# Attention and two expert layers on one core: the first batch's sums of four and its pooled part move from VectorE into TensorE's products

## The chip, the cores and the metric

The kernel runs on one core of a Trainium2 chip. The metric is the device time of one execution in microseconds (us). TensorE (PE, with its weight loads as PEld), VectorE (DVE), ScalarE (ACT), GpSimd (POOL) and SyncE (SP) each run their own instructions in order; DMA transfers are issued on queues of SP and of ACT.

## The reference, cut to what matters

```python
# q, k, v: 4 batches x 8 heads x 576 tokens x 64
q_d, k_d, v_d = (t.reshape(B, H, 144, 4, D).mean(axis=3) for t in (q, k, v))
out_d = softmax(scale * q_d @ k_d^T) @ v_d                 # 144 pooled tokens
out_up = np.repeat(out_d, 4, axis=2)                       # the pooled part, back on 576
mask = np.abs(pos[:, None] - pos[None, :]) < 4
out_local = softmax(where(mask, scale * q @ k^T, -1e9)) @ v
x = (out_up + out_local) as [2304 tokens, 512]
x = ((x @ w_a) * (x @ w_b)) @ w_out                        # 512 -> 1536 -> 512
h = x @ w_in                                               # 512 -> 2048
out = (h * clip(h + 3, 0, 6) / 6) @ w_out2                 # 2048 -> 512
```

## The kernel before, in words

The program has three phases, each of which a small list scheduler writes out: `Plan` (lines 57 to 135) holds steps with an engine, an estimated duration, a due time (`want`), the steps they follow, and the tags they take and give back (buffers and banks, with caps). It simulates the engines and calls each step's function in the order in which it would start, and each engine then runs its instructions in that order; on the chip only the order counts. Changed durations, due times or takes therefore change the order around them too.

Phase 1 makes x and multiplies it with w_a and w_b. The 2304 tokens are cut into units of 116 tokens (five to a batch, the last of 112), and the units into seven token blocks of 2, 3, 3, 3, 3, 3 and 3 units. `BUFS` (line 175) gives two score tiles `s2` of two PSUM banks each and four single banks `b`; the cap `pv` lets one result of a value product at a time hold one of those four.

`pooled(b, g, want)` does the pooled attention of one pair of heads g of batch b, four groups to a batch. `load` brings queries and keys (tile qk), `load_v` the values as four slices, one for each of the four neighbours of a pooled token. `add_v` (lines 375 to 379) adds the four slices with two DVE instructions. `sums` (381 to 384) adds four neighbouring queries and keys in one DVE reduce, into dqk. `score` (386 to 393, result dsc) multiplies summed queries with summed keys on PE, four F32 matmuls of two instructions each. `top` takes the maxima (line 397) and scales them (400), `exps` is on ACT (406), `inverse` (412, 413) and `norm` (345) on DVE; `turn` transposes on PE (424, dpt), `turned` copies on ACT (431, deT), `pv` (434 to 439, dpo) multiplies with the added values, and `keep` (444) writes the result to od.

`local(u, want)` does the windowed attention of unit u in the same steps: `score` (mask at 479, products at 485, result sc), `top` (493, 494), `exps` (501; eight heads in one step), `inverse`, `norm`, `turn` (516), `turned` (520), and `pv` (528; 32 instructions into po, each with its own start). `total` (536) adds the pooled part from od, each value repeated four times, into xf on DVE; `x_first` (543, ACT) and `x_second` (546, DVE) split xf into a rounded part and its remainder, tile x, as PE multiplies those in pairs.

`decode` (223 to 280) turns one slab of weights, 128x1024 numbers of 64 bits (raw), into two such parts (wh): ACT at line 237, DVE at 243, 244, 248, 254, 255 and 261, ACT at 265, DVE at 268. `job(n, f)` (568) multiplies block n with slab f: 12 products of w_a and 12 of w_b (578, pab), their product on ACT and DVE (584, 587), and the store. The first six jobs are blocks 0 to 2 with the slabs 0 and 1; then come the slabs from 2 on with the blocks 0 to 2, and later the other blocks. The first two slabs are loaded by ACT's queue (lines 945 and 946 give `queue=nc.scalar`), the others by SP's.

Phase 2 multiplies with w_out, and phase 3 is the second expert layer.

## Time and profile before

| | us |
|---|---|
| median of 3 runs (lowest, highest) | 973.01 (971.87, 974.76) |
| the profiled execution | 975.95 |
| its span, first to last instruction | 974.2 |
| PE busy in the span | 927.7 |
| DVE busy | 766.0 |
| ACT busy | 457.3 |

How to read it: the span is one execution as the profiler recorded it; the difference to that execution's time lies around the program. Busy times overlap, as the engines work side by side. PEclk is the clock that PE was granted, as a share of full speed. A wait in brackets at a row's end is the idle time of that engine just before the row, and what ended it.

### The profile page before, as it was taken

The page shows a single profiled execution, that of the slowest core. Times are in us where ns is not written, and L with a number is a line of the kernel's source. Part 1 is how long each engine was busy: PE and PEld are TensorE (multiplying, and loading weights), DVE is VectorE, ACT ScalarE, POOL GpSimd, SP SyncE. Part 2 cuts the span into 40 slices and gives each one's busy share as a digit, 9 for nine tenths or more (in the row PEclk, how much of TensorE's full clock was granted, in tenths as well). Part 3 has the DMA queues.
Part 4 walks back from the last instruction along what each step waited for, and adds up shares of the span by engine and source line. Part 5 has one row for each costly group of instructions (what it writes and reads, how often), then busy time and mean ns, then how long its engine had stood idle before and what let it go on. Part 6 is the DMA issues. An engine that isn't in the chain of part 4 may idle for free.

```text
span 974.2 us, 18526 instructions
## 1 busy us (share of the span) xinstructions
PE 927.7 (95%) x7040; PEld 869.7 (89%) x7040; DVE 766.0 (79%) x1390; ACT 457.3 (47%) x1164; POOL 5.2 (1%) x44
## 2 busy tenths in 40 slices
PE   3779999999999999999999898999999999999998
PEld 2568899999989999997877688999999999999998
DVE  6888898954746959686887644899898999997983
ACT  3765633445455424224444333545454665554551
POOL 1000000000000000000000000000000000000000
PEclk9988999999999999999999899999999999999999
DMA  8442755323314433325678664334327891815401
GB/s 259 173 122 82 243 163 192 127 84 99 112 49 132 169 136 133 131 95 204 214 241 271 219 211 147 104 142 164 122 108 256 274 295 43 265 39 167 159 17 49
DMA packets 90089, 151.21 MB, mean 155 GB/s; under 512 B 8208, under 2 KB 71696, under 8 KB 85648
## 3 DMA queue, kind: packets, MB, share of 16 engines
q1 hardware_dynamic: 80384, 132.54, 41.4%
q10 hardware_dynamic: 9616, 17.49, 5.7%
q8 instruction: 55, 0.90, 0.4%
q14 instruction: 34, 0.28, 0.1%
HBM read 100.19 MB, written 49.81 MB: 154 GB/s over the span
## 4 chain that ended last, share of the span: by engine, by line
PE 80%; DVE 9%; DMA 7%; ACT 2%; issue 2%; ACTq 0%; SPq 0%; DVEq 0%
PE pab L578 32%; PE ph L747 16%; PE oacc L870 15%; PE acc L635 9%; DMA h<-h_d 4%; PE po L528 2%; DVE in L678 2%; DMA vz<-vt 1%; PE sc L485 1%; PE pt L516 1%; PE dpo L439 1%; DVE e L843 1%; DVE w2o L1078 1%; PE dpt L424 1%; DMA raw<-wab 1%
## 5 line engine op out<-in xcount | busy, mean ns | idle before, releaser
L578 PE MATMUL pab<-x,wh 128*128 128x344 f32 (+2 forms) x2016 | 325.6, 320 | 1.9 <-DVE wh L268 1.7
L578 PEld LDWEIGHTS pab<-x,wh 128*128 128x128 f32 x2016 | 311.8, 192 | 4.7 <-DVE wh L268 2.0
L870 PE MATMUL oacc<-w2o,in 128*128 128x256 f32 x1512 | 182.1, 283 | 1.4 <-DVE in L678 1.4
L870 PEld LDWEIGHTS oacc<-w2o,in 128*128 128x128 f32 x1512 | 181.3, 191 | 2.2 <-DVE in L678 2.0
L747 PE MATMUL ph<-in,w 128*128 128x384 f32 x1008 | 177.3, 337 | 2.5 <-ACT in L675 2.3
L747 PEld LDWEIGHTS ph<-in,w 128*128 128x128 f32 x1008 | 176.7, 189 | 3.0 <-ACT in L675 2.5
L635 PE MATMUL acc<-h,wo 128*128 128x512 f32 (+1 forms) x720 | 156.5, 377 | 9.4 <-ACT h L623 8.3
L635 PEld LDWEIGHTS acc<-h,wo 128*128 128x128 f32 x720 | 126.7, 191 | 39.2 <-ACT h L623 10.8
L763 DVE TENSOR_TENSOR part<-ph,part 128x384 f32<-128x384 f32 x168 | 85.7, 549 | 9.6 <-PE ph L747 8.8
L584 ACT ACTIVATE a<-pab 128x344 f32<-128x344 f32 (+2 forms) x84 | 37.3, 447 | 95.8 <-PE pab L578 67.5
L771 ACT ACTIVATE r<-part,three 128x384 f32<-128x384 f32 x96 | 56.5, 613 | 52.9 <-DVE part L763 50.1
L587 DVE TENSOR_TENSOR a<-a,pab 128x344 f32<-128x344 f32 (+2 forms) x84 | 41.4, 493 | 50.3 <-PE pab L578 45.2
L627 DVE TENSOR_TENSOR h<-h 128x512 fp32r<-128x512 f32 (+1 forms) x60 | 37.4, 634 | 51.6 <-ACT h L623 51.3
L675 ACT ACTIVATE in<-gr 128x384 fp32r<-128x384 f32 x96 | 47.5, 521 | 41.0 <-PE oacc L870 31.2
L237 ACT ACTIVATE m<-raw 128x1024 f32<-128x1024 f32 x34 | 39.3, 1157 | 57.0 <-DVE raw L255 21.2
L623 ACT ACTIVATE h<-h 128x512 fp32r<-128x512 f32 (+1 forms) x60 | 34.9, 588 | 64.5 <-DMA h<-h_d 51.6
L678 DVE TENSOR_TENSOR in<-gr,in 128x384 fp32r<-128x384 f32 x96 | 49.5, 551 | 6.7 <-ACT in L675 6.2
L675 ACT ACTIVATE in<-e 128x384 fp32r<-128x384 f32 x72 | 36.5, 527 | 33.9 <-PE oacc L870 20.2
L774 DVE SCALAR_TENSOR_TENSOR r<-r,part 128x384 f32<-128x384 f32 x96 | 50.4, 548 | 1.2 <-ACT r L771 1.1
L501 ACT ACTIVATE e<-sc,mx 128x64 f32<-128x64 f32 x160 | 47.6, 328 | 5.5 <-DVE mx L494 4.4
L255 DVE SCALAR_TENSOR_TENSOR raw<-raw,m 128x1024 f32<-128x1024 uint32 x34 | 41.7, 1227 | 1.2
L261 DVE TENSOR_TENSOR raw<-raw 128x1024 f32<-128x1024 f32 x34 | 41.5, 1221 | 0.5
(82 smaller groups left out, 885.7 us busy)
## 6 DMA issues: line engine op xcount, KB each, us to landing
g_d<-r SPq DMA_DIRECT2D x96, 192.0 KB
gr<-g_d SPq DMA_DIRECT2D x48, 384.0 KB
h<-h_d ACTq DMA_DIRECT2D x48, 256.0 KB
raw<-wab SPq DMA_DIRECT2D x10, 1024.0 KB
h_d<-a SPq DMA_DIRECT2D x48, 172.0 KB
raw<-w2i SPq DMA_DIRECT2D x8, 1024.0 KB
raw<-w2o SPq DMA_DIRECT2D x8, 1024.0 KB
qk<-qk SPq DMA_DIRECT2D x14, 576.0 KB
```

The source lines that it names most:

```text
L255: nc.vector.scalar_tensor_tensor(out=lo.bitcast(F32), in0=lo, scalar=2.0 ** -52, in1=m, op0=ALU.mult, op1=ALU.mult)
L261: nc.vector.tensor_tensor(v, v, lo.bitcast(F32), op=ALU.add)
L501: nc.scalar.activation(e[:, p, h], L["s4"][:, p, h], AF.Exp, bias=L["mx"][:, p, h:h + 1], scale=SCALE, accum_out=z[:, p, h:h + 1])
L578: nc.tensor.matmul(T[k], wab_t[f][:, x, c], xs[n][:, g, y, :nb], start=(g == 0 and i == 0), stop=(g == KC - 1 and i == 2))
L635: nc.tensor.matmul(accs[n][e], wo_t[f // 2][:, x, c], hs[n, f][:, y], start=(f == 0 and i == 0), stop=(f == F1 - 1 and i == 2))
L675: nc.scalar.activation(x[0][:, 0], src(), AF.Copy)
L678: nc.vector.tensor_tensor(x[0][:, 1], src(), x[0][:, 0], op=ALU.subtract)
L747: nc.tensor.matmul(acc[k], t[:, x, g * P:(g + 1) * P], X[k, g][0][:, y], start=(g == 0 and n == 0), stop=(g == 1 and n == 2))
L763: nc.vector.tensor_tensor(s[name], acc[k], s[other], op=ALU.add)
L771: nc.scalar.activation(T["r"], src(), AF.Relu, bias=three)
L774: nc.vector.scalar_tensor_tensor(out=T["r"], in0=T["r"], scalar=6.0, in1=src(), op0=ALU.min, op1=ALU.mult)
L870: nc.tensor.matmul(acc[n][e], X[n, k][0][:, x, e * P:(e + 1) * P], t[:, y], start=(k == 0 and i == 0), stop=(k == K - 1 and i == 2))
```

## The change

For batch 0 (`soon` in `pooled`): the four value slices aren't added, and `pv` multiplies with each of them into the same bank (16 matmuls in place of 4). DVE sums the keys alone (128x144 in place of 128x288 results), and `score` takes the four query slices as weights one after another, read with a step of four numbers (16 matmuls in place of 4). For the units of 116 tokens in blocks 0 to 2 (seven units; `soon` in `local`): `pv` begins with one product of the identity with the pooled part, read from od with each column four times (128x464), the 32 others add to it, `total` isn't done, and `x_first` and `x_second` read PSUM. For every unit the exponentials are four steps of two. The first two slabs of w_a and w_b go on SP's queue. Some durations, due times and takes of the planner change with it.

```diff
--- before.py
+++ after.py
@@ -353 +353 @@
-    def pooled(b, g, want):
+    def pooled(b, g, want, soon):
@@ -377 +377 @@
-            T["v"] = v_[:, :, 0] if b == 0 else slot(ap, [HD, 2, P], F32, "dv", "dv")
+            T["v"] = slot(ap, [HD, 2, P], F32, "dv", "dv")
@@ -380,0 +381,3 @@
+        def tokens():
+            return qks[b, g][:, :, HALO:HALO + S].rearrange("p a (s r) -> p a s r", r=FACTOR)
@@ -381,0 +385,2 @@
+            a = slice(1, 2) if soon else slice(0, 2)
@@ -383,2 +388 @@
-            nc.vector.tensor_reduce(T["s"], qks[b, g][:, :, HALO:HALO + S].rearrange("p a (s r) -> p a s r", r=FACTOR),
-                                    axis=AX.X, op=ALU.add)
+            nc.vector.tensor_reduce(T["s"][:, a], tokens()[:, a], axis=AX.X, op=ALU.add)
@@ -390,4 +394,6 @@
-                for h in range(2):
-                    r = slice(64 * h, 64 * h + 64)
-                    nc.tensor.matmul(sc[:HD, h, a * SD:(a + 1) * SD], s[r, 0, a * HD:(a + 1) * HD], s[r, 1],
-                                     start=True, stop=True)
+                part = slice(a * HD, (a + 1) * HD)
+                for i in range(FACTOR if soon else 1):
+                    for h in range(2):
+                        r = slice(64 * h, 64 * h + 64)
+                        nc.tensor.matmul(sc[:HD, h, a * SD:(a + 1) * SD], tokens()[r, 0, part, i] if soon else s[r, 0, part],
+                                         s[r, 1], start=(i == 0), stop=(not soon or i == FACTOR - 1))
@@ -435,0 +442,2 @@
+            v = [T["v_"][:, :, i] for i in range(FACTOR)] if soon else [T["v"]]
@@ -437,3 +445,5 @@
-                for h in range(2):
-                    r = slice(64 * h, 64 * h + 64)
-                    nc.tensor.matmul(po[r, :SD], T["v"][:, c, r], T["eT", c][:, h], start=(c == 0), stop=(c == 1))
+                for i, x in enumerate(v):
+                    for h in range(2):
+                        r = slice(64 * h, 64 * h + 64)
+                        nc.tensor.matmul(po[r, :SD], x[:, c, r], T["eT", c][:, h], start=(c == 0 and i == 0),
+                                         stop=(c == 1 and i == len(v) - 1))
@@ -449,2 +459,2 @@
-        av = DVE(dve(768) + 0.06, want - 3, add_v, [lv], take=[] if b == 0 else ["dv"], give=[] if b == 0 else ["vraw"])
-        i = DVE(dve(2 * S), want, sums, [ld], take=["dqk"])
+        av = lv if soon else DVE(dve(768) + 0.06, want - 1, add_v, [lv], take=["dv"], give=["vraw"])
+        i = DVE(dve(S if soon else 2 * S), want, sums, [ld], take=["dqk"])
@@ -452 +462 @@
-        i = PE(0.5, want, score, [i], take=["s2"], give=["dqk"])
+        i = PE(2.0 if soon else 0.5, want, score, [i], take=["s2"], give=["dqk"])
@@ -454 +464 @@
-        i = ACT(4 * 0.47, want, exps, [i], take=["de"], give=["s2"])
+        i = ACT(4 * 0.37, want, exps, [i], take=["de"], give=["s2"])
@@ -457,4 +467,5 @@
-        t = [PE(0.3, want, turn(c), [i], take=["b", "turn"], give=["de"] if c else []) for c in range(2)]
-        t = [ACT(act(2 * SD), want, turned(c), [t[c]], take=["deT"], give=["b", "turn"]) for c in range(2)]
-        i = PE(0.6, want, pv, [*t, av], take=["b", "pv"], give=["deT", "deT", "wh" if b == 0 else "dv"])
-        S_["od", b, g] = ACT(act(SD), want, keep, [i, S_.get(("od", b, 0))], take=[] if g else ["od"], give=["b", "pv"])
+        t = [PE(0.3, want, turn(c), [i], take=["b", "turn", "deT"], give=["de"] if c else []) for c in range(2)]
+        t = [ACT(act(2 * SD), want, turned(c), [t[c]], give=["b", "turn"]) for c in range(2)]
+        i = PE(1.6 if soon else 0.6, want, pv, [*t, av], take=["b", "pv"] + ([] if g else ["od"]),
+               give=["deT", "deT", "wh" if b == 0 else "vraw" if soon else "dv"])
+        S_["od", b, g] = ACT(act(SD), want, keep, [i, S_.get(("od", b, 0))], give=["b", "pv"])
@@ -462 +473 @@
-    def local(u, want):
+    def local(u, want, soon):
@@ -496,4 +507,5 @@
-        def exps():
-            e = L["e"] = slot(ap, [P, HP, 2, KB], F32, "e", "e")
-            z = L["z"] = ap.tile([P, HP, 2], F32, tag="z", bufs=2, name="z")
-            for p in range(HP):
+        def exps(p):
+            def run():
+                if p == 0:
+                    L["e"] = slot(ap, [P, HP, 2, KB], F32, "e", "e")
+                    L["z"] = ap.tile([P, HP, 2], F32, tag="z", bufs=2, name="z")
@@ -501,2 +513,3 @@
-                    nc.scalar.activation(e[:, p, h], L["s4"][:, p, h], AF.Exp, bias=L["mx"][:, p, h:h + 1],
-                                         scale=SCALE, accum_out=z[:, p, h:h + 1])
+                    nc.scalar.activation(L["e"][:, p, h], L["s4"][:, p, h], AF.Exp, bias=L["mx"][:, p, h:h + 1],
+                                         scale=SCALE, accum_out=L["z"][:, p, h:h + 1])
+            return run
@@ -524,0 +538,2 @@
+            if soon:
+                nc.tensor.matmul(L["po"].rearrange("p a (s r) -> p a s r", r=FACTOR), ident, pooled_part(), start=True, stop=False)
@@ -529 +544,4 @@
-                                         L["eT"][:, p, i * KB:i * KB + QB], start=True, stop=True)
+                                         L["eT"][:, p, i * KB:i * KB + QB], start=not soon,
+                                         stop=(not soon or (p == HP - 1 and i == 1)))
+            if soon:
+                L["xf"] = L["po"]
@@ -531,2 +549 @@
-        def total():
-            xf = L["xf"] = slot(ap, [P, HP, UT], F32, "xf", "xf")
+        def pooled_part():
@@ -535 +552,4 @@
-            up = ods[b][:, :, c:c + n].unsqueeze(3).to_broadcast([P, HP, n, FACTOR])
+            return ods[b][:, :, c:c + n].unsqueeze(3).to_broadcast([P, HP, n, FACTOR])
+        def total():
+            xf = L["xf"] = slot(ap, [P, HP, UT], F32, "xf", "xf")
@@ -537 +557,2 @@
-                                    L["po"][:, :, :tokens].rearrange("p a (s r) -> p a s r", r=FACTOR), up, op=ALU.add)
+                                    L["po"][:, :, :tokens].rearrange("p a (s r) -> p a s r", r=FACTOR), pooled_part(),
+                                    op=ALU.add)
@@ -549 +570 @@
-        ld = DMA(128, want - 25 if u < 2 else want - 5, load, [S_.get(("pv", u - 2))])
+        ld = DMA(128, want - 20 if u < 2 else want - 5, load, [S_.get(("pv", u - 2))])
@@ -555 +576,2 @@
-        i = ACT(8 * 0.42, want, exps, [i], take=["e"], give=["s2"])
+        for p in range(HP):
+            i = ACT(2 * 0.31, want, exps(p), [i], take=[] if p else ["e"], give=["s2"] if p == HP - 1 else [])
@@ -558,5 +580,7 @@
-        i = PE(0.5, want, turn, [i], take=["b", "turn"], give=["e"])
-        i = ACT(act(n), want, turned, [i], take=["eT"], give=["b", "turn"])
-        i = S_["pv", u] = PE(0.9, want, pv, [i, ld], take=["b", "pv"], give=["eT"])
-        i = DVE(dve(n), want, total, [i] + [S_["od", b, g] for g in range(HP)], take=["xf"],
-                give=["b", "pv"] + (["od"] if last else []))
+        i = PE(0.5, want, turn, [i], take=["b", "turn", "eT"], give=["e"])
+        i = ACT(act(n), want, turned, [i], give=["b", "turn"])
+        ods_ = [S_["od", b, g] for g in range(HP)]
+        i = S_["pv", u] = PE(1.7 if soon else 0.9, want, pv, [i, ld] + ods_,
+                             take=["b", "pv"] + ([] if soon else ["xf"]), give=["eT"])
+        if not soon:
+            i = DVE(dve(n), want, total, [i], give=["b", "pv"] + (["od"] if last else []))
@@ -565 +589 @@
-        S_["x2", u] = DVE(dve(n), want, x_second, [i], give=["xf"])
+        S_["x2", u] = DVE(dve(n), want, x_second, [i], give=["b", "pv"] if soon else ["xf"])
@@ -941,2 +965,2 @@
-                pooled(u // NU, g, t - 0.05 + 0.01 * g)
-        local(u, t)
+                pooled(u // NU, g, t - 0.05 + 0.01 * g, u // NU < 1)
+        local(u, t, m < 3 and unit_tokens(u) == UT)
@@ -946 +970 @@
-                                queue=nc.scalar if f < 2 else None)
+                                queue=None)
```

SP's queue at the start of the program (v0 are the value slices of batch 0, raw the slabs of weights, vz the values of a unit, qk the queries and keys, those of batch 1 here). Before:

```order
L370 DMA v0_146<-vd 72x1024
L370 DMA v0_156<-vd 72x1024
L370 DMA v0_161<-vd 72x1024
L370 DMA v0_178<-vd 72x1024
L473 DMA vz0_105<-vt 64x512 x2
L473 DMA vz1_106<-vt 64x512 x2
L365 DMA qk_279<-qk 128x2x576
L365 DMA qk_303<-qk 128x2x576
```

With the change:

```order
L370 DMA v0_176<-vd 72x1024
L370 DMA v0_183<-vd 72x1024
L370 DMA v0_210<-vd 72x1024
L370 DMA v0_215<-vd 72x1024
L229 DMA raw_248<-wab 128x1024
L229 DMA raw_312<-wab 128x1024
L484 DMA vz0_105<-vt 64x512 x2
L484 DMA vz1_106<-vt 64x512 x2
L365 DMA qk_391<-qk 128x2x576
```

The two slabs, which ACT's queue issued before, stand between the values of batch 0 and those of the first two units.

PE's first rows (dsc is a pooled score, dpt a transpose of its exponentials, dpo the pooled product with the values, sc a unit's score; qk_113, qk_117, qk_121 and the last one are the four groups of batch 0). Before:

```order
L392 MATMUL dsc<-dqk 72x144 x16
L424 MATMUL dpt<-ident,de 72x72 x8
L439 MATMUL dpo<-deT,v_146 64x144 x4
L424 MATMUL dpt<-ident,de 72x72 x4
L479 LDWEIGHTS ident_88
L479 MATMUL sc<-mask_sb,ident_88 128x256
...
L485 MATMUL sc<-qk_132 64x64 x4
L424 MATMUL dpt<-ident,de 72x72 x4
L439 MATMUL dpo<-deT,v_156 64x144 x4
```

With the change:

```order
L398 MATMUL dsc<-dqk,qk_113 72x144 x16
L398 MATMUL dsc<-dqk,qk_117 72x144 x16
L398 MATMUL dsc<-dqk,qk_121 72x144 x16
L430 MATMUL dpt<-ident,de 72x72 x4
L490 LDWEIGHTS ident_88
L490 MATMUL sc<-mask_sb,ident_88 128x256
...
L496 MATMUL sc<-qk_144 64x64 x4
L430 MATMUL dpt<-ident,de 72x72 x4
L448 MATMUL dpo<-deT,v_176 64x144 x16
L398 MATMUL dsc<-dqk,qk_144 72x144 x16
```

Before, one row holds the scores of all four groups; with the change each group has a row, and the fourth stands behind a unit's score and the first group's product with the values.

DVE's rows behind the second pooled maximum's (dmx) scale, up to the maximum of the fourth group. Before:

```order
L383 TENSOR_REDUCE dqk<-qk_132 128x288
L378 TENSOR_TENSOR v_146<-v_146 72x2x256
L379 TENSOR_TENSOR v_146<-v_146 72x2x128
L378 TENSOR_TENSOR v_156<-v_156 72x2x256
L379 TENSOR_TENSOR v_156<-v_156 72x2x128
L345 TENSOR_TENSOR de<-de,dz 72x576
L378 TENSOR_TENSOR v_161<-v_161 72x2x256
L379 TENSOR_TENSOR v_161<-v_161 72x2x128
L378 TENSOR_TENSOR v_178<-v_178 72x2x256
L379 TENSOR_TENSOR v_178<-v_178 72x2x128
...
L397 TENSOR_REDUCE dmx<-dsc 72x4
```

With the change:

```order
L345 TENSOR_TENSOR de<-de,dz 72x576
L388 TENSOR_REDUCE dqk<-qk_144 128x144
...
L403 TENSOR_REDUCE dmx<-dsc 72x4
L406 TENSOR_SCALAR dmx<-dmx 72x4
L345 TENSOR_TENSOR de<-de,dz 72x576
L504 TENSOR_REDUCE mx<-sc 128x8
L505 TENSOR_SCALAR mx<-mx 128x8
...
L345 TENSOR_TENSOR de<-de,dz 72x576
L403 TENSOR_REDUCE dmx<-dsc 72x4
```

The eight rows of value adds are gone, the sum is half as large, and the first unit's maximum (mx) and a third norm (de) stand ahead of the fourth group's maximum. Behind PE's row 370 or so (377 with the change), and DVE's 404 (389), the two orders are the same on every engine.

## Rows read from the trace of the kernel before

**Rows 1.** The page: one engine's busy time, share of the span, instructions.

```profile
PE 927.7 (95%) x7040; PEld 869.7 (89%) x7040; DVE 766.0 (79%) x1390; ACT 457.3 (47%) x1164; POOL 5.2 (1%) x44
```

**Rows 2.** Windows: stretch and its length in us, busy time by engine, clock, DMA.

```profile
core 0: us, PE busy (x) PEld busy (x) DVE busy (x) ACT busy (x) POOL busy (x), PEclk, DMA share, GB/s
0.00:30.00 30.00, 12.53 (x104) 8.15 (x104) 18.51 (x35) 10.40 (x42) 3.97 (x28) 1.00 0.91 284
6.00:22.70 16.70, 8.02 (x52) 5.45 (x53) 13.91 (x26) 5.20 (x26) 0.00 (x0) 1.00 0.98 262
22.70:54.30 31.60, 21.75 (x304) 15.64 (x307) 27.36 (x53) 22.13 (x95) 0.00 (x0) 0.95 0.55 184
54.30:114.70 60.40, 55.36 (x670) 49.24 (x662) 52.52 (x96) 37.98 (x164) 0.64 (x8) 0.88 0.41 130
114.70:442.00 327.30, 327.30 (x2789) 315.21 (x2790) 240.31 (x388) 138.78 (x405) 0.64 (x8) 1.00 0.39 128
```

**Rows 3.** Timeline of the start: us, duration, engine, line, work [idle before it <-releaser].

```profile
5.32 2.85 DVE L383 TENSOR_REDUCE dqk<-qk 128x288 f32<-128x1152 f32 x2 [4.46 <-DMA qk<-qk]
6.73 0.80 PEld L392 LDWEIGHTS dsc<-dqk 64*72 64x72 f32 x8 [6.73 <-DVE dqk L383]
6.73 1.24 PE L392 MATMUL dsc<-dqk 64*72 64x144 f32 x8 [6.73 <-DVE dqk L383]
...
21.78 0.75 DVE L397 TENSOR_REDUCE dmx<-dsc 72x4 f32<-72x576 f32 x1
...
26.91 1.12 ACT L237 ACTIVATE m<-raw 128x1024 f32<-128x1024 f32 x1 [3.58 <-DMA raw<-wab]
...
28.06 0.69 DVE L243 TENSOR_SCALAR m<-m 128x1024 f32<-128x1024 f32 x1 [2.55 <-ACT m L237]
```

**Rows 4.** The chain of waits, pieces in order of time: start us, us, what.

```profile
18.95 7.94 DMA raw<-wab
...
28.32 1.44 ACT de L406 x8
...
62.43 0.64 PE dsc L392 x8
...
75.90 1.96 PE pab L578 x12
...
85.89 0.67 PE sc L485 x32
```

**Rows 5.** Timelines of PE and DVE around two cuts, the x halves of units 1 and 7.

```profile
43.51 1.96 PE L528 MATMUL po<-eT,vz 128*64 128x58 f32 x32 [0.69 <-ACT eT L520]
...
47.94 1.16 PE L528 MATMUL po<-eT,vz 128*64 128x58 f32 x32
...
53.74 0.59 DVE L546 TENSOR_TENSOR x<-xf,x 128x464 fp32r<-128x464 f32 x1
...
114.00 0.63 DVE L546 TENSOR_TENSOR x<-xf,x 128x464 fp32r<-128x464 f32 x1
...
114.69 1.55 PE L578 MATMUL pab<-x,wh 128*128 128x348 f32 x8 [0.16 <-DVE x L546]
```

**Rows 6.** Tiles v, qk and xf: duration ns min/median/max, first and last start us, forms.

```profile
L378 DVE TENSOR_TENSOR v<-v x4: 679/680/681, 15.1 to 18.9; 72x512 f32<-72x512 f32 x4
L379 DVE TENSOR_TENSOR v<-v x4: 420/420/422, 15.8 to 19.6; 72x256 f32<-72x256 f32 x4
...
L383 DVE TENSOR_REDUCE dqk<-qk x10: 1319/1344/1354, 5.3 to 126.6; 128x288 f32<-128x1152 f32 x10
...
L536 DVE TENSOR_TENSOR xf<-po,od x20: 612/640/643, 45.6 to 308.4; 128x464 f32<-128x464 f32 x16, 128x448 f32<-128x448 f32 x4
...
L546 DVE TENSOR_TENSOR x<-xf,x x20: 590/632/643, 48.4 to 309.7; 128x464 fp32r<-128x464 f32 x16, 128x448 fp32r<-128x448 f32 x4
```

**Rows 7.** DVE's groups by line, 54.3 to 114.7 us: busy us, mean ns, idle before.

```profile
L536 DVE TENSOR_TENSOR xf<-po,od 128x464 f32<-128x464 f32 (+1 forms) x6 | 3.8, 633 | 2.3 <-PE po L528 2.1
...
L587 DVE TENSOR_TENSOR a<-a,pab 128x232 f32<-128x232 f32 (+1 forms) x8 | 3.6, 450 | 4.6 <-PE pab L578 4.6
```

More of the change, by code (lines that the diff above doesn't have):

```diff
@@ L528, in pv @@
                         nc.tensor.matmul(L["po"][64 * h:64 * h + 64, p, i * QB:(i + 1) * QB], v_[:, h, i, p],
-                                         L["eT"][:, p, i * KB:i * KB + QB], start=True, stop=True)
+                                         L["eT"][:, p, i * KB:i * KB + QB], start=not soon,
[3 more added lines that the diff above has]
+        def pooled_part():
+            n = tokens // FACTOR
+            c = j * UT // FACTOR
+            return ods[b][:, :, c:c + n].unsqueeze(3).to_broadcast([P, HP, n, FACTOR])
         def total():
             xf = L["xf"] = slot(ap, [P, HP, UT], F32, "xf", "xf")
-            n = tokens // FACTOR
-            c = j * UT // FACTOR
-            up = ods[b][:, :, c:c + n].unsqueeze(3).to_broadcast([P, HP, n, FACTOR])
             nc.vector.tensor_tensor(xf[:, :, :tokens].rearrange("p a (s r) -> p a s r", r=FACTOR),
-                                    L["po"][:, :, :tokens].rearrange("p a (s r) -> p a s r", r=FACTOR), up, op=ALU.add)
+                                    L["po"][:, :, :tokens].rearrange("p a (s r) -> p a s r", r=FACTOR), pooled_part(),
+                                    op=ALU.add)
         def x_first():
```

## The prediction

> **What bounds the kernel now.** I read the page first, then the windows, then the start of the timeline. The page says that PE works for 95% of the span [rows 1], but a share over the whole span hides the stage in which the change lies. The windows cut it up [rows 2]: from 114.7 to 442 us PE is busy for 327.30 of 327.30 us, so there only PE's own work counts. Before that it isn't the bound: from 22.7 to 54.3 us DVE is busy for 27.36 of 31.60 us against PE's 21.75, and from 54.3 to 114.7 DVE for 52.52 of 60.40 against PE's 55.36, a PE that ran part of this at the lower clock (mean 0.88). So the head of the program is bound by DVE and by the way through the first transfers, and what ends earlier there lets PE's unbroken stretch begin earlier.
>
> The timeline of the start shows the links [rows 3]. DVE sums the first two groups from 5.32 us, PE waits 6.73 us for them, the fourth group's maximum is taken at 21.78, and then ACT waits 3.58 us and DVE 2.55 us for the first weight slab. The chain gives that slab's transfer 7.94 us from 18.95 on [rows 4]. The head ends where the last unit of the third block is split into its two x halves (114.00 us plus 0.63), and PE starts behind exactly that [rows 5].
>
> **The yardstick.** The sum is made against the profiled execution, 975.95 us (span 974.2), which lies 2.94 us above the median of the runs, 973.01; I take the difference that I work out from that median. A measurement of this kernel tells about 0.3% (2.9 us) from no change.
>
> **What DVE loses.** The four value adds go: 4 × (0.68 + 0.42) = 4.4 us [rows 6]. The four sums of batch 0 halve: 4 × 0.67 = 2.7 us of 1.344 each [rows 6]. Seven adds of the pooled part go: 7 × 0.64 = 4.5 us [rows 6]. Together 11.6 us.
>
> **What PE gains.** A score goes from 8 to 32 instructions, a pooled product from 8 to 32, four of each: 192 more. At the lower level 8 of them take 1.24 us (155 ns each) [rows 3], at the upper 0.64 us (80 ns) [rows 4]: 15.4 us in the end if the upper level holds, 29.8 if not. The seven identity products (128x464, F32) have no row. Below, 12 products of 344 columns in 1.96 us [rows 4] give 0.22 us for 464 columns, twice that for an F32 product in two passes: 0.44. Above, a pair of 144 columns costs 0.16 us, and if no two of those overlapped, 464 columns cost 0.52; twice that, as the pairs use half of the array each, is 1.03. I take 0.8, nearer to the F32 row: 5.6 us. PE thus gains about 21 us. This work hides in PE's idle time: 114.7 us hold some 59 us of work at the upper level (my estimate: the 85 us that PE was busy, with what ran at the lower level counted half), and with 18 us more by then it still fits into the 100 us from PE's first product to the point found below. That cover is gone if the lower level stays; that is the first rival.
>
> **Step A, up to the fourth group's maximum.** Half a sum less: PE begins at 6.73 − 0.68 = 6.05. The first score is 32 × 155 ns = 4.96, to 11.0. PE then has been at work without a gap for 5 us and has the second score ready behind it. In the trace the level rose so: the 32 products at 43.51 took 1.96 us, PE had no gap from there on, and at 47.94 the same 32 took 1.16 [rows 5]. I take the upper level from 11.0 on. Second score 2.56, to 13.6; the third finds its bank freed by the first group's exponentials (11.0 + 0.92 for the maximum + 1.5; one group's four took some 1.44 [rows 4]) and ends at 16.2. Then by the new order a local score (0.67 [rows 4] and its mask, 1.0), eight turns (at most 80 ns each, 0.64), half a microsecond for a copy, the first pooled product (2.56) and the fourth score (2.56): 23.5. Maximum and scale, 0.92: 24.4. Before it was 21.78 + 0.92 = 22.7. Step A **loses 1.7 us**.
>
> **Step B, to the x halves of unit 1** (before: 53.74 + 0.59 = 54.3 [rows 5]). Before, the stretch was 31.6 us, of which 2.55 waited for the slab, so 29.1 remain. Out of it fall two pooled-part adds (1.3), the norm and inverse of the third group and the maximum of unit 0, which now stand ahead of the cut (1.0 and 0.8), and one value add of batch 1, which moves behind it (1.1). Into it come one local norm (0.7) and one sum of batch 1 (1.3). That is 26.9, and 0.5 for small waits: 24.4 + 27.4 = 51.8, which **gains 2.5 us**. The slab is not waited for on this count. It now goes on SP right behind the values, whose last add began at 18.9 [rows 6], so they had landed by then; the slab's 1.05 MB then take 3.7 us at the 284 GB/s of the first 30 us [rows 2], landing by 22.6, while ACT reaches its first pass at about 24.3. The far bound is the old 7.94 us counted from 18.9, landing at 26.8 and 2.5 us lost again. The transfers moved behind it (unit values, batch 1) are not used before 40 us, since the first value product of a unit is at 43.51 [rows 5].
>
> **Step C, to the x halves of the third block.** Before 60.3 us. DVE's work falls by 5.7: five adds (3.2), a norm and a sum already done (0.7 and 1.3), the maximum of unit 8 now behind (0.8), 0.3 back for an inverse. Of the 6.9 us in which DVE waited for PE here [rows 7], 2.3 stood before the adds that go; the split halves inherit that wait by way of ACT, so I take only 0.6 off. The end is 51.8 + 60.3 − 6.3 = 105.8, against 114.6: **8.8 us earlier**.
>
> **What PE has left then.** By the order one block of 12 products (1.96 [rows 4]) and unit 8's score (0.95) now stand behind that point instead of ahead of it: 2.9 us given back. The mean clock of 0.88 from 54.3 to 114.7 [rows 2] shows that the level fell at pauses; where they lie in the new order can't be worked out, and I allow one more such fall, at the 0.8 us that the 32 products lost at 43.51 against 47.94 [rows 5]. From there on both orders agree, PE has no idle time to 442 [rows 2], and the gain goes through to the end. Sum: −8.8 + 2.9 + 0.8 = **−5.1 us**, 970.9 on the profiled execution and 967.9 on the median. The exponentials in four steps cost nothing: the same instructions, and ACT is busy for 22.13 of 31.60 us [rows 2]; the finer steps only let a copy go between two of them. A changed order of takes has no instruction of its own either.
>
> **Rivals.** *First, slower: the lower clock level stays through the start.* For it: PE stands at that level for the first 43 us now, and the new order has gaps of a microsecond at 16 to 20. Then four scores take 4 × 4.96, the first pooled product 4.96 and the rest 3.5: the fourth maximum ends at some 35 instead of 24.4, the decoding of the slab behind it starts 11 us later, and −5 + 11 gives +6: 979. It decides if 64 products in a row, 9.9 us, do not raise the level. Against it: PE was busy for only 8.02 us in the 16.7 from 6 to 22.7 [rows 2]; now nothing is missing between the first two scores.
>
> *Second, no change: the query slices as weights.* Each weight load now reads every fourth number of a row. Eight loads of adjacent numbers take 0.80 us [rows 3], 100 ns each, beside products of 155 ns, so 55 ns of cover. If a strided load takes twice as long, each of the 32 costs 45 ns at the lower level and about half at the upper: 1.4 us for the first score, 0.7 to 1.4 for the others, all on step A's path: 3.6 to 5.8 us, and the time comes to about 972.5. The Trainium skill ("SBUF — State Buffer", section "Specifications (TRN2)") speaks for it: it gives lines of 16 bytes, wants two hits in each for full bandwidth, and charges each crossing, while a step of four F32 numbers crosses at every one. No row here loads weights with a step, so the trace neither bears it out nor denies it.
>
> *Third, no change: the bank.* The pooled part in PE's bank means that the bank is free only after the second x half, 2.8 us after the start of the add that freed it before (first rows 45.6 and 48.4 [rows 6]). If PE waits that long behind two of the seven units, 5.6 us come back: 973.5. For it speaks that the planner lets one bank of this kind be in use at a time (its cap pv), so the next value product is put behind the second x half; against it, that PE has the products of the blocks to do meanwhile.
>
> **How the numbers follow.** Forecast 0.58, first rival 0.14, second 0.12, third 0.16. The forecast's own spread is 961 (all 11.6 us and the 2.55 of waiting gained, less step A's loss) to 970; below that little can lie, as no more is removed. The slower side takes in the first rival: 961 to 979. Faster by over 0.3% (under 970.1) is the forecast with a little taken off, 0.57; within 0.3% are the second and third rivals for the most part, 0.25; slower 0.18.
>
> **What would show it.** Right: PE's first score at about 6.1 us and 5 us long, the second half as long; the fourth maximum near 24; no wait for the first slab; PE's unbroken stretch from about 106 us; the third block's x at 106. Wrong at once: later scores at 5 us each (first rival), weight loads of L398 above 150 ns at either level (second), PE idle before L448 or L529 for a release by DVE (third), the slab still waited for by ACT at 27 us (step B), or 114 to 442 us no longer full.

## The result, and the profile after

The changed kernel takes 963.54 us (median of 4 runs, 962.63 to 964.64) against 972.44 for the kernel before. The recorded ratio of all the runs, which isn't the quotient of these two medians, is 0.9894, 95% interval 0.9868 to 0.9919. In a second comparison it came to 961.81 against 974.29, ratio 0.9873 (0.9843 to 0.9903). The forecast was 967.9 (961 to 979), a gain of 5.1 us where the medians give 8.9 and 12.5: the right way, and too small. Two executions of the experiments lie far outside and are compared with nothing: one of query_sums_dve, the profiled one (1022.94 us at a mean clock of 0.849), and one of relief_only (2540.63 us).

The page's line of the engines, after:

```profile
PE 931.3 (97%) x7246; PEld 873.2 (91%) x7246; DVE 754.6 (78%) x1375; ACT 456.2 (47%) x1164; POOL 5.6 (1%) x44
```

The windows of the head, after:

```profile
6.00:22.70 16.70, 15.88 (x240) 14.62 (x240) 9.80 (x24) 8.44 (x45) 0.00 (x0) 1.00 1.03 297
22.70:54.30 31.60, 27.60 (x384) 20.96 (x378) 30.16 (x51) 23.99 (x102) 0.00 (x0) 0.84 0.65 198
54.30:114.70 60.40, 60.02 (x720) 52.85 (x717) 57.17 (x102) 36.17 (x129) 1.04 (x8) 1.00 0.46 147
```

The column behind POOL is the clock. It counts as 1.00 up to the first change of level that a trace recorded: the rise to the upper level (2.4 GHz), at 48.0 us in the kernel before and at 10.6 with the change. So the 1.00 that [rows 2] shows up to 22.7 us says nothing of the level, and 0.84 can't be set against the 0.95 there; ahead of the first record, only the durations tell the level. Behind it the records have the lower level (1.2 GHz) four times between 51.4 and 109.5 us before, and once with the change, from 34.5 to 44.8.

Against [rows 1, 2]: DVE has lost 11.4 us in all, as worked out (11.6). The row to look at is the last. From 54.3 to 114.7 PE is now busy for 60.02 of 60.40 us at a mean clock of 1.00, where it was 55.36 at 0.88. PE is all but unbroken from about 49 us on, not from 106, so from there on PE is the bound and no longer DVE. The start, in the timeline:

```profile
6.35 6.36 PE L398 MATMUL dsc<-dqk,qk 64*72 64x144 f32 x64 [6.35 <-DVE dqk L388]
...
13.18 2.41 PE L398 MATMUL dsc<-dqk,qk 64*72 64x144 f32 x32 [0.47 <-ACT de L412]
...
21.69 0.75 DVE L403 TENSOR_REDUCE dmx<-dsc 72x4 f32<-72x576 f32 x1 [1.35 <-PE dsc L398]
...
22.42 1.14 ACT L237 ACTIVATE m<-raw 128x1024 f32<-128x1024 f32 x1
...
23.17 2.18 PE L448 MATMUL dpo<-deT,v 72*64 72x144 f32 x32
...
24.40 0.69 DVE L243 TENSOR_SCALAR m<-m 128x1024 f32<-128x1024 f32 x1
...
48.56 0.63 DVE L567 TENSOR_TENSOR x<-po,x 128x464 fp32r<-128x464 f32 x1
...
97.17 0.63 DVE L567 TENSOR_TENSOR x<-po,x 128x464 fp32r<-128x464 f32 x1
```

The first slab is not waited for any more: the pass at 22.42 has no release by a DMA behind it, and DVE's at 24.40 no idle time, against 3.58 and 2.55 us [rows 3]. The two rows of L567 are the cuts of the prediction, the x halves of units 1 and 7: 49.2 and 97.8 us at their ends against 54.3 and 114.6 [rows 5]. DVE's groups by line from 54.3 to 114.7:

```profile
L611 DVE TENSOR_TENSOR a<-a,pab 128x232 f32<-128x232 f32 (+2 forms) x10 | 4.6, 462 | 0.9 <-PE pab L602 0.6 <-issue 0.3
...
L556 DVE TENSOR_TENSOR xf<-po,od 128x448 f32<-128x448 f32 (+1 forms) x2 | 1.2, 624 | 0.0
```

DVE's idle time before the groups that wait for PE, 6.9 us in this stretch [rows 7], is down to 0.9 (6.7 and 0.6 of it are put down to PE itself). The totals of single executions spread by 4 us and more, so the experiments are read by a mark that parts can't blur: the start of the last block product of the first phase, which the view of that one line gives as its last start. Before and after:

```profile
L578 PE MATMUL pab<-x,wh x2016: 267/321/653, 55.0 to 441.5; 128*128 128x344 f32 x105, 128*128 128x348 f32 x53, 128*128 128x232 f32 x26
```

```profile
L602 PE MATMUL pab<-x,wh x2016: 267/321/431, 51.2 to 430.1; 128*128 128x344 f32 x104, 128*128 128x348 f32 x52, 128*128 128x232 f32 x28
```

By this mark the first phase ends 11.4 us earlier. The profiled execution of the second comparison has 430.0.

### The profile page after: what moved, and what is told of

Read it like the earlier page. It is cut to its first block, busy times and chain, and to the rows that moved or that the text cites. A ratio compares the mean times of both kernels' runs of the same rounds, so it can differ in the third digit from the quotient of the medians.

```text
span 962.2 us, 18892 instructions
## 1 busy us (share of the span) xinstructions
PE 931.3 (97%) x7246; PEld 873.2 (91%) x7246; DVE 754.6 (78%) x1375; ACT 456.2 (47%) x1164; POOL 5.6 (1%) x44
## 4 chain that ended last, share of the span: by engine, by line
PE 81%; DVE 8%; DMA 7%; ACT 2%; issue 1%; ACTq 0%; SPq 0%; DVEq 0%
PE pab L602 32%; PE ph L771 18%; PE oacc L894 14%; PE acc L659 7%; DMA h<-h_d 5%; PE po L543 2%; PE dsc L398 2%; DVE in L702 1%; DMA gr<-g_d 1%; PE sc L496 1%; PE dpo L448 1%; PE pt L529 1%; DVE raw L248 1%; DVE h L651 1%; DMA raw<-w2o 1%
## 5 line engine op out<-in xcount | busy, mean ns | idle before, releaser
L602 PE MATMUL pab<-x,wh 128*128 128x344 f32 (+2 forms) x2016 | 319.8, 317 | 0.1
L602 PEld LDWEIGHTS pab<-x,wh 128*128 128x128 f32 x2016 | 306.4, 188 | 3.6 <-issue 1.8
L659 PEld LDWEIGHTS acc<-h,wo 128*128 128x128 f32 x720 | 125.8, 190 | 40.9 <-ACT h L647 11.7
L651 DVE TENSOR_TENSOR h<-h 128x512 fp32r<-128x512 f32 (+1 forms) x60 | 37.4, 635 | 52.4 <-ACT h L647 52.2
L513 ACT ACTIVATE e<-sc,mx 128x64 f32<-128x64 f32 x160 | 48.1, 321 | 5.3 <-DVE mx L505 5.3
L255 DVE SCALAR_TENSOR_TENSOR raw<-raw,m 128x1024 f32<-128x1024 uint32 x34 | 41.7, 1227 | 1.2
L248 DVE SCALAR_TENSOR_TENSOR raw<-raw,m 128x1024 uint32<-128x1024 uint32 x34 | 41.5, 1221 | 0.2
```

The lines of the kernel that those rows point to most:

```text
L248: nc.vector.scalar_tensor_tensor(out=hi, in0=hi, scalar=0xC0000000, in1=T["m"].bitcast(U32), op0=ALU.bitwise_and, op1=ALU.bitwise_or)
L513: nc.scalar.activation(L["e"][:, p, h], L["s4"][:, p, h], AF.Exp, bias=L["mx"][:, p, h:h + 1], scale=SCALE, accum_out=L["z"][:, p, h:h + 1])
L602: nc.tensor.matmul(T[k], wab_t[f][:, x, c], xs[n][:, g, y, :nb], start=(g == 0 and i == 0), stop=(g == KC - 1 and i == 2))
L651: nc.vector.tensor_tensor(h[:, 1], h[:, 1].bitcast(F32), h[:, 0], op=ALU.subtract)
L659: nc.tensor.matmul(accs[n][e], wo_t[f // 2][:, x, c], hs[n, f][:, y], start=(f == 0 and i == 0), stop=(f == F1 - 1 and i == 2))
```

## The experiments

The marks of all runs, each from its own profile (x 1 and x 7 are the ends of those units' x halves), with the recorded ratio to the kernel before:

| run | x 1 | x 7 | last product | ratio (95%) |
|---|---|---|---|---|
| before | 54.3 | 114.6 | 441.5 | 1 |
| the change | 49.2 | 97.8 | 430.1 | 0.9894 (0.9868 to 0.9919) |
| change_again | 49.0 | 97.6 | 430.0 | 0.9873 (0.9843 to 0.9903) |
| before_slab_sp | 51.0 | 106.8 | 433.7 | 0.9954 (0.9928 to 0.9981) |
| slab_on_act | 53.8 | 102.6 | 434.9 | 0.9934 (0.9900 to 0.9968) |
| ballast | 65.2 | 126.2 | 453.1 | 1.0117 (1.0073 to 1.0161) |
| relief_only | 46.8 | 96.2 | 428.5 | 0.9890 (0.9858 to 0.9923) |
| adjacent_weights | 48.7 | 97.3 | 429.6 | 0.9901 (0.9874 to 0.9928) |
| value_adds_dve | 50.5 | 99.1 | 431.4 | 0.9942 (0.9921 to 0.9962) |
| query_sums_dve | | | | 0.9934 (0.9911 to 0.9958) |
| query_sums_dve_2 | 51.7 | 100.2 | 432.6 | 0.9942 (0.9919 to 0.9965) |
| both_sums_dve | 50.9 | 99.5 | 431.8 | 0.9926 (0.9898 to 0.9953) |
| pooled_part_dve | 48.1 | 104.6 | 432.2 | 0.9929 (0.9907 to 0.9951) |
| pool_adds | 50.5 | 110.6 | 432.1 | 0.9916 (0.9886 to 0.9947) |

Two things can be read off the table. First, the one line that moves the slabs brings 7.8 of the 11.4 us by itself, in the kernel before (before_slab_sp); the moved sums, the pooled part and the new order add 3.6. Second, eight runs keep the changed order of DVE and PE: the change, change_again, slab_on_act, relief_only, adjacent_weights, value_adds_dve, query_sums_dve_2 and both_sums_dve. In all of them x 7 comes 48.5 to 49.4 us behind x 1 and the last product 332.3 or 332.4 behind x 7, and no fall of the level is recorded between x 1 and x 7. In the order before, with its level falling, the first of these stretches is 55.8 to 61.0 us and the second 326.9. So whatever is taken back in the changed order, the slab included, has its price ahead of x 1, and what lies behind came with the changed order.

**TensorE's added work without DVE's relief.** In the kernel before, in the score (and alike in the value product), and in the units:

```diff
-                for h in range(2):
+                for i in range(FACTOR if b == 0 else 1):
+                    for h in range(2):
...
+            if m < 3 and tokens == UT:
+                nc.tensor.matmul(L["po"], ident, L["eT"][:, :, :UT], start=True, stop=True)
```

> The kernel before, with its order and all its DVE work, plus idle repetitions on TensorE of the size that the change adds: batch 0's scores and value products are done four times each (the repetition restarts the sum), and the seven units get a 128x464 identity product that is overwritten. Theory A (the busier TensorE keeps its clock level, so DVE waits less for block products): no fall of the clock from 54 to 115 us (mean 0.97 or more against 0.88), the third block's x done at 104 to 111 us against 114.6, total 966 to 971 against 972.4. Theory B (the gain is DVE's relief of 11.6 us; the clock only follows): third block's x at 114 to 119 us, total 973 to 979.

Slower, and by more than either theory said: the phase ends 11.6 us later. The timeline of PE and ACT shows what came between, and a window the level:

```profile
19.72 2.23 PE L441 MATMUL dpo<-deT,v 72*64 72x144 f32 x32 [0.25 <-ACT deT L432]
...
27.43 1.12 ACT L237 ACTIVATE m<-raw 128x1024 f32<-128x1024 f32 x1 [3.41 <-DMA raw<-wab]
...
28.90 3.63 PE L441 MATMUL dpo<-deT,v 72*64 72x144 f32 x28 [3.53 <-ACT deT L432]
...
37.63 4.11 PE L441 MATMUL dpo<-deT,v 72*64 72x144 f32 x32
```

```profile
30.00:50.00 20.00, 16.80 (x198) 13.99 (x196) 15.68 (x28) 9.01 (x42) 0.00 (x0) 0.50 0.28 86
```

The added scores did raise the level: 32 value products take 2.23 us at 19.7. Then ACT waits 3.41 us for the slab, the copy deT stands behind that wait in ACT's order, and PE stands still for 3.53 us. The records have the lower level from 25.5 us, where this pause begins, to 56.2; the same 32 products take 4.11 there, and from 30 to 50 us the mean clock is 0.50. So work added to PE is cheap only where the level holds behind it; theory A, that busier is faster by itself, falls.

**DVE's relief without TensorE's added work.** In the changed kernel, one slice of each four and no pooled part:

```diff
-                for i in range(FACTOR if soon else 1):
+                for i in range(1):
...
-            v = [T["v_"][:, :, i] for i in range(FACTOR)] if soon else [T["v"]]
+            v = [T["v_"][:, :, i] for i in range(1)] if soon else [T["v"]]
...
-                nc.tensor.matmul(L["po"].rearrange("p a (s r) -> p a s r", r=FACTOR), ident, pooled_part(), start=True, stop=False)
```

> The changed kernel and its order without TensorE's added products (one query slice and one value slice instead of four, no pooled part: these parts of the result are left out). Theory A: TensorE pauses again, the clock falls in the stretch 54 to 115 us (mean under 0.95), and although 21 us of TensorE work are gone the total is 961 to 967 against the change's 963.5. Theory B: TensorE's relief counts where it is the bound, five identity products from 49 us on (3.9 us) and some of the start; clock as with the change; total 956 to 960.

```profile
54.30:114.70 60.40, 58.29 (x715) 52.99 (x714) 56.98 (x97) 36.76 (x129) 0.94 (x8) 1.00 0.47 150
```

The windows have one row for that stretch. The clock doesn't fall (1.00), against theory A, though the total, 962.9, lies in its range. Taking away all of the 21 us brings 1.6 us by the mark, not the 3.9 and more of theory B. The 1.6 is a net figure: the first record of the upper level is at 51.5 us in this run and at 10.6 with the change, so without the added products the start runs at the lower level. So far PE's added work is hidden almost whole, as the prediction had it.

**The slabs back on ACT's queue, all else as changed.**

```diff
-                                queue=None)
+                                queue=nc.scalar if f < 2 else None)
```

> The changed kernel with the first two weight slabs issued by ACT's queue again, the order of all else the same. If the slab's wait is one of the things that went: ACT gets the slab at about 27 us again in place of 22.4, DVE waits 2 to 4 us for it, and as TensorE is bound without a pause only from 49 us on, most of it lasts: total 965 to 967.5 against 963.5. If it is hidden by what DVE and ACT have to do meanwhile: 963 to 964.

```profile
18.77 0.35 ACTq L229 DMA_DIRECT2D raw<-wab  x1
...
19.16 0.41 ACT L437 ACTIVATE deT<-dpt 72x288 f32<-72x288 f32 x1 [3.26 <-DMA vz<-vt]
...
26.52 1.14 ACT L237 ACTIVATE m<-raw 128x1024 f32<-128x1024 f32 x1 [1.00 <-DMA raw<-wab]
```

The phase ends 4.8 us later. The slab's own wait is only 1.00 us here. The larger one is the issue: a copy that PE needs stands behind it in ACT's order, and ACT is idle for 3.26 us ahead of that copy. The profile puts the wait down to the landing of the unit values vz; why the issue came so late isn't shown further. PE pauses for 1.81 us, the records have the lower level from 19.95 to 23.36 us, and the fourth maximum is taken at 24.68 us in place of 21.69. The total is 966.1, and its interval takes in both theories; the mark decides for the first.

**The kernel before with nothing changed but the slabs' queue.**

```diff
-                                queue=nc.scalar if f < 2 else None)
+                                queue=None)
```

> The kernel before with one thing changed: the first two weight slabs are issued by SP's queue, the slots in the order as the planner sets them. The changed kernel with its slabs on ACT's queue lost 4.8 us at the end of the first phase, more than the 2.55 us that DVE waited before. Theory C (the slab's late landing starts a row of waits and a fall of the clock, worth 4 to 6 us whatever else is changed): x of unit 1 done at 49 to 51 us against 54.3, end of the first phase 4 to 6 us earlier than 441.8. Theory D (it is worth the wait alone, as DVE's other work fills the time): x of unit 1 at 51.5 to 52.5, end of the phase 1.5 to 2.5 us earlier.

Theory C, and beyond it: the phase ends 7.8 us earlier by this one line. 3.3 us are there at x of unit 1. The other 4.5 come from there to x of unit 7, where the order and the work of DVE and PE are those of the kernel before. Its windows and DVE's groups over just that stretch, 51.0 to 106.9:

```profile
51.00:106.90 55.90, 50.85 (x666) 45.18 (x658) 52.18 (x95) 37.72 (x164) 0.64 (x8) 0.95 0.44 140
```

```profile
L536 DVE TENSOR_TENSOR xf<-po,od 128x464 f32<-128x464 f32 (+1 forms) x6 | 3.8, 632 | 1.0 <-PE po L528 0.8
...
L587 DVE TENSOR_TENSOR a<-a,pab 128x232 f32<-128x232 f32 (+1 forms) x8 | 3.6, 447 | 1.7 <-PE pab L578 1.7
```

DVE does the same work (52.18 us against 52.52 [rows 2]), but its idle time before the groups that wait for PE is 2.7 us in place of 6.9 [rows 7], and the mean clock is 0.95 in place of 0.88. The stretch is 4.5 us shorter and DVE waits 4.2 us less. With the same order and work, then, the waits went as the time at the lower level did; which of the two made the other this run doesn't tell.

**The single sums and adds back on DVE**, the order of all else as changed. Value adds, behind the group's norm, and one product of the added slices:

```diff
+                nc.vector.tensor_tensor(v_[:, :, 0:2], v_[:, :, 0:2], v_[:, :, 2:4], op=ALU.add)
+                nc.vector.tensor_tensor(T["v"], v_[:, :, 0], v_[:, :, 1], op=ALU.add)
...
-            v = [T["v_"][:, :, i] for i in range(FACTOR)] if soon else [T["v"]]
+            v = [T["v"]]
```

> The changed kernel with the four value adds of batch 0 on DVE again, each behind its group's norm (4.4 us more for DVE, 96 products less for TensorE), the order of all else the same. Theory C (DVE sets the start): x of unit 1 at 51 to 54 us against 49.2, end of the first phase 2 to 4.5 us later than the change's 430.4. Theory D (DVE had gaps beside the scores that take the adds): x of unit 1 at 48.5 to 50, end of the phase within 1 us.

The end comes 1.3 us later, x of unit 1 1.3 us: between the theories. Of 4.4 us more for DVE 3.1 don't show; whether gaps took them or PE's 96 products less paid for them can't be told apart here. Queries summed on DVE, four matmuls to a score:

```diff
-            a = slice(1, 2) if soon else slice(0, 2)
+            a = slice(0, 2)
...
-                for i in range(FACTOR if soon else 1):
+                for i in range(1):
...
```

> The changed kernel with batch 0's queries summed on DVE again (2.7 us more for DVE, 96 products less for TensorE), the order of all else the same. Theory C: DVE sets the start, x of unit 1 1.5 to 2.7 us later. Theory D: the scores are TensorE's own chain there, 32 products of 2.2 to 4.2 us each in place of 0.6 to 1.2, so the fourth maximum comes 2 to 4 us earlier and x of unit 1 0 to 2 us earlier than 49.2; the change's query adds are then of no use, total 961 to 963.5.

The median, 968.29 us, is against theory D's 961 to 963.5. The marks come from a second run of the same kernel:

> As query_sums_dve, whose profiled execution ran at a clock of 0.849 throughout. Theory C (DVE sets the start): x of unit 1 at 50.7 to 52 us against 49.2, first phase's end 1 to 2.5 us later than 430.4. Theory D (the scores are TensorE's chain there, so fewer of its products pay for the sums): x of unit 1 at 47 to 49.2, end of the phase 0 to 2 us earlier.

Theory C by its numbers (x of unit 1 2.5 us later, the end 2.5), though the fourth maximum is taken at 21.64 us, as with the change (21.69). What differs is the level. PE's timeline:

```profile
24.79 4.11 PE L448 MATMUL dpo<-deT,v 72*64 72x144 f32 x32
...
30.30 1.13 PE L496 MATMUL sc<-qk 64*64 64x64 f32 x32
...
32.42 0.75 PE L496 MATMUL sc<-qk 64*64 64x64 f32 x32
```

Without the long scores in front the level rises only at 32.6 us by the records, and the value products, 4.11 us each 32 here, take 2.18 with the change. So the query adds on PE seem to pay partly as warming.

Both together, the two edits in one kernel:

> The changed kernel with the value adds and the query sums of batch 0 both on DVE again, the order of all else the same; what stays of the change is the pooled part on TensorE, the slabs on SP's queue and the new order. If the parts add up (value adds 1.3 us by their run, query sums by the run beside this): first phase ends 1 to 4 us later than the change's. If one hides the other: not later than the worse of the two.

With both on DVE the phase ends 1.7 us later, less than with the query sums alone (2.5) and far less than the sum, 3.8: the parts don't add up. The level rises only at 46.7 us here, so a likely reason, not tested by itself, is that there are no added products left that the lower level could double. The pooled part on DVE for all units, with a new order by the planner:

```diff
-        local(u, t, m < 3 and unit_tokens(u) == UT)
+        local(u, t, False)
```

> The changed kernel with the pooled part added by DVE for all units as before (seven adds of 0.64 us more for DVE, seven identity products of 0.78 us less for TensorE; the planner sets the order anew). Theory C: DVE, busy for 57 of 60 us from 54 to 115, is lengthened by 3.2 us there and the clock falls again in pauses of TensorE: end of the first phase 3 to 6 us later. Theory D: TensorE is bound without pauses from 49 us on, so five identity products less give 3.9 us back and DVE's work fits in: end of the phase 0 to 3 us earlier, total 960 to 963.5.

2.1 us later at the end, between the theories. x of unit 7 comes 6.8 us later than with the change, but x of unit 4 4.5 us earlier, so the new order is mixed into it and DVE's part can't be read alone.

**Weights from adjacent numbers.** One argument of the score's products:

```diff
-tokens()[r, 0, part, i] if soon else
+qks[b, g][r, 0, HALO + (4 * a + i) * HD:HALO + (4 * a + i + 1) * HD] if soon else
```

> The changed kernel with batch 0's query slices read as 72 adjacent numbers in place of every fourth (the pooled scores of batch 0 are then other numbers). If a load of weights with a step costs more: 32 loads take 1.9 us or less at the upper level in place of 2.2, scores end earlier, total lower by 0.5 to 4 us. If not: loads and total as with the change, 963 to 964.5.

The loads of these weights and the fourth score, first with adjacent numbers, then with the change:

```profile
L398 PEld LDWEIGHTS dsc<-dqk,qk x128: 136/140/242, 6.1 to 21.0; 64*72 64x72 f32 x128
19.23 2.18 PE L398 MATMUL dsc<-dqk,qk 64*72 64x144 f32 x32
```

```profile
L398 PEld LDWEIGHTS dsc<-dqk,qk x128: 203/219/241, 6.3 to 21.2; 64*72 64x72 f32 x128
19.23 2.42 PE L398 MATMUL dsc<-dqk,qk 64*72 64x144 f32 x32
```

The step does cost something, as the first theory had it: a load has a median of 219 ns against 140 (smallest, median and largest stand behind the count), and the fourth score, at the upper level in both, takes 2.42 us against 2.18. The largest loads, 241 and 242 ns, are alike, so nothing shows at the lower level. x of unit 1 and the end come 0.5 us earlier with adjacent numbers. That run's level rose 1.4 us later (12.0 us against 10.6), so its first scores can't be set beside those of the change.

**A version to go further: batch 1's value adds on GpSimd.**

```diff
+            adder = nc.gpsimd if b == 1 else nc.vector
...
```

> A version that goes further: the changed kernel with the four value adds of batch 1 (1.1 us of DVE each, three of them ahead of x of unit 2) on GpSimd, which is busy for 5.6 us in all. Theory C (DVE sets the start until 49 us): x of unit 1 at 46.5 to 48.5, first phase's end 0.5 to 2.5 us earlier. Theory D (from 49 us on TensorE has no pauses, so DVE's relief changes its order alone): x of unit 1 up to 2 us earlier, the end within 0.5 us of 430.4. If GpSimd's adds slow DVE beside them: DVE's mean in that stretch above 1.23 us for 128x1024 numbers, and the end later.

```profile
53.79 1.80 POOL L379 TENSOR_TENSOR vraw<-vraw 72x512 f32<-72x512 f32 x1 [10.34 <-DMA vraw<-vd]
...
54.48 2.20 DVE L255 SCALAR_TENSOR_TENSOR raw<-raw,m 128x1024 f32<-128x1024 uint32 x1
```

Later by 2.0 us at the end. DVE's L255, which reads two tensors of SBUF, takes 2.20 us beside GpSimd's add here and 1.23 without (with the change). The planner also put a sum of queries ahead of unit 1's x halves in the gap. Of the versions that compute the same result, none ends its first phase ahead of the change. The change itself once more:

> The changed kernel itself once more, beside the three below on one chip, as totals of the runs so far spread by 4 us and more while the end of the first phase tells parts apart to a microsecond. If the gain is the head's alone: first phase ends at 430 to 431, ratio to before 0.987 to 0.991. If part of the first result was luck behind the first phase: ratio 0.992 to 0.996 with the same end of the phase.

The head is the same to 0.2 us, the total lower by another 1.7 us: the gain is not luck behind the first phase.

## Why the prediction was right, and where it was too small

**What bounds it: right for the kernel before.** DVE and the first transfers set the head, PE's own work the rest. With the change PE is the bound from 49 us on, not from 106. relief_only shows that PE's 21 us more cost 1.6 net.

**Step A, 24.4 us forecast, 22.65 measured** (21.69 and 0.96 for maximum and scale). The level rose where it was said to, about the end of the first score (10.6 us by the records, 11.0 forecast). A piece of the chain, after:

```profile
6.35 4.16 PE dsc L398 x32
```

The first score took 4.16 us, the second 6.36 − 4.16 = 2.2. The price of a product was off: 1.24 and 0.64 us for 8 contain the tail of the last, so 155 and 80 ns were taken where rows of 32 show 130 and 70 to 75. Over four scores and a value product that is 1.8 us, as much as the 1.7 that step A was forecast too long.

**Step B, 27.4 us forecast, 26.5 measured.** The work that was counted out was right to 0.9 us, and the slab was not waited for, though the level did fall once more in this stretch (from 34.5 to 44.8 us). But the slab's price was taken as the 2.55 us that DVE waited, and by the runs it is 4.8 us in the change's order and 7.8 in the order before. In the change's order 3.0 of it are there at the fourth maximum, behind the issue that ACT waits for; in the order before the larger half, 4.5, comes after x of unit 1.

**Step C is the term with the largest error: 54.0 us forecast, 48.6 measured.** DVE's own work fell as counted, from 52.4 us between the two cuts to 46.7 (5.7 both forecast and measured). "Of the 6.9 us in which DVE waited for PE here, ... I take only 0.6 off", and 0.8 us were set aside for one more fall of the level. In fact the waits went to 0.9 and the level didn't fall at all: some 6 us of waiting gone in place of 0.6. The prediction read the waits as fixed, a product that is late because it stands late, and took the level to fall once more. The runs show that waits and level go together: before_slab_sp has the order and work of the kernel before, and its waits went from 6.9 to 2.7 as the clock went from 0.88 to 0.95. They show too that a late x of unit 1 doesn't bring them back: slab_on_act has it at 53.8 us, as late as before, and takes 48.8 us to x of unit 7 with no fall of the level. So the 48.6 us belong to what the eight runs share, most likely the new order, which was not run by itself, and the prediction counted what the order moves past its cuts, but no gain from it.

**What PE had left: 3.7 us forecast, 5.4 measured** (16.8 us at x of unit 7, 11.4 at the end of the phase). With PE full from 49 us on, x of unit 7 is no longer what PE waits for, so an earlier x 7 is in part only order: the stretch behind it is 5.4 us longer in all eight runs of the changed order. The errors don't cancel: A, B and C were each forecast too long, 8.0 us together, and 1.7 of it is given back here, so the 5.1 us forecast became 11.4 by the mark.

**The rivals.** The first (the lower level stays) didn't come here, but it is real and was priced too low: ballast comes nearest to it, in the order before, 11.6 us later at the end of the phase. Its point of decision wasn't the 64 products, which raised the level in both, but whether the level holds behind them; in ballast it is lower again from 25.5 us on, where PE's pause begins, so the slab's move belongs to the added products. The second is real and small. Its sign, loads of L398 above 150 ns, is there (219 ns), but at the upper level alone, and it costs 0.24 us a score where 3.6 to 5.8 us for all were priced; adjacent_weights gives 0.5 us in all. The Trainium skill ("SBUF — State Buffer", section "Specifications (TRN2)") charges a crossing of 16-byte lines, and this trace agrees for loads of 72 weights at the upper level. Of the third nothing shows: PE has 0.4 us of idle time from 54.3 to 114.7.

**What stays open.** By the medians each of the sums and adds taken back costs 2.5 to 5.5 us, by the end of the first phase 1.3 to 2.5. The rest would have to lie behind it, where the time differs from one execution to another (below); single profiles don't settle it. The stretch from x of unit 1 to x of unit 7 is 11.7 us shorter with the change, of which 5.4 are given back behind it. The 6.3 that stay came with the new order, the pooled part on PE and the exponentials in steps together: no run had the new order without the rest, and pooled_part_dve was ordered anew, so none of them has a price of its own. Whether the waits make the level fall or the level makes the waits is argued from timelines; no run held the level fixed.

## What to carry to other kernels

A wait in an engine's order can cost more than the idle time it shows, here 4.8 and 7.8 us for 2.55: look at what stands behind the waiting instruction, a DMA issue too, who needs that, and whether TensorE is at its lower level behind the pause. Work can be moved onto TensorE almost free while another engine bounds the stage (1.6 us for some 21 here), if the level holds behind it; work of that size in the order before, with all of DVE's work kept, cost 11.6 us. Where waits for TensorE lie in a stretch with a mean clock well under 1, don't take them as fixed: here they went with the clock. And when a change brings a new order with it, give the order a run of its own, or its share can't be told from the rest.

## What the runs showed of the hardware

Eight products of 1.24 us don't mean 155 ns each: 16 and 32 of 144 columns took 2.19 and 4.11 us at the lower level, which is 120 ns for each one more, and 0.71 us for 8 (PE's timeline before, at 62.36 us) and 2.18 for 32 at the upper level give 61. The rest of a row, some 0.28 and 0.22 us, is read here as the tail of the last product.

Weights read with a step of four F32 numbers took a median of 219 ns a load against 140 for adjacent ones, at the upper level alone (adjacent_weights).

A DVE instruction with two inputs in SBUF was slowed by GpSimd's adds: 2.20 us against 1.23 (pool_adds). The Trainium skill says so ("SBUF — State Buffer", section "Who interferes with whom"), and this trace agrees.

Behind the first phase two executions of the same program differ by 4.9 us. PE's group of the products with w_out in 430 to 620 us, first in the change's profile, then in that of change_again:

```profile
L659 PE MATMUL acc<-h,wo 128*128 128x512 f32 (+1 forms) x720 | 155.7, 375 | 11.0 <-ACT h L647 9.0 <-DVE h L651 2.0
```

```profile
L659 PE MATMUL acc<-h,wo 128*128 128x512 f32 (+1 forms) x720 | 155.2, 375 | 7.3 <-ACT h L647 6.0 <-DVE h L651 1.1
```

The spans are 962.2 and 957.1 us with the first phase alike. PE waits 11.0 or 7.3 us for h, which comes back by DMA: 3.7 of the 4.9 us. The two profiles come from two comparisons, so the chip may have a part in it. That spread hides a few microseconds of any change in the head, so marks inside the profile tell more than totals.
